# A recurrence and two MLPs on one core: the weight conversion as six lagged stages, the second MLP's weights kept in SBUF, and a mask product taken by VectorE from PSUM

## Chip, core and metric

The kernel runs on one core of a Trainium2 chip. The metric is the device time of one execution in microseconds (us). The core's engines are TensorE (PE, its weight loads PEld), VectorE (DVE), ScalarE (ACT), GpSimd (POOL) and SyncE (SP, which here only issues DMAs). Each engine works through its own queue in program order; they meet at semaphores.

## The reference

Three steps follow each other. A recurrence over 768 time steps for 4 batches of 8 heads with 40 channels, then two MLPs over its 3072 rows of 320 columns:

```python
for t in range(S):
    y[:, :, t] = einsum('bhd,bhde->bhe', rt, state)
    Sa = einsum('bhde,bhe->bhd', state, at)
    state = state * wt[:, :, None, :] - einsum('bhd,bhe->bhde', Sa, bt) + einsum('bhd,bhe->bhde', vt, kt)
...
h = x @ moe_w_in;  x = (maximum(h, 0) ** 2) @ moe_w_out            # 320 -> 2048 -> 320
h = x @ moe2_w_in; out = (h * clip(h + 3, 0, 6) / 6) @ moe2_w_out
```

The weights come as 64-bit floats. The kernel gets them as pairs of 32-bit words (low word, high word) and has to turn each pair into a 32-bit float itself.

## The kernel before

**The recurrence** is cut into 12 chunks of 64 steps with 4 batches each: 48 units, `i` = 0 to 47. In the main loop one iteration treats one unit; its words come from `ORDER` (`ORDER0` until the first MLP has input). Products of decayed rows for unit `i + 8` are made in `f1` (L581, eight matmuls): `f1a` copies one half to `TB`, which goes to DRAM (`DT`) and feeds a triangular inverse; `f1b` treats the other half: ScalarE copies 64x256 out of the bank to `RK` (L595), GpSimd multiplies it there by a mask (L596). It is done 96 times, twice for each unit; the first eight units go through it ahead of the loop. A chunk's inverse (`inv_gen`, L627 and L630, 62 small steps in a row on VectorE) is spread over the loop by `tick()`; only that of chunk 1 runs on GpSimd. `ys` (L710, L713 on PE, then L717, L719, L722 on VectorE) gives the rows of a unit.

**The MLPs** run in *pieces*. Their tokens are six groups of 512, the 2048 hidden columns 16 blocks of 128: 96 blocks for each MLP. An "in" piece multiplies one block into the hidden layer (L221 to L225), applies the function (first MLP L235 to L239, second L230 to L239); an "out" piece multiplies it with the second weight and adds it up (first L248 to L252, second L260 to L262). Operands are taken in a high and a low part, so that each product is three. The word `M` of the order calls `fill`, which issues one piece (or `keep_warm`, matmuls that nobody reads, where there is none), then up to five ticks, and two steps of the conversion. The first MLP begins in iteration 9; four `M` in an iteration make two blocks. After the loop pieces follow each other without recurrence; the first MLP's last group and all of the second MLP run there.

**The conversion** (`convert`, a generator) turns 32 items (16 blocks of both weights, 128x384 or 128x320) of one MLP. An item goes through VectorE (L127, L135), ScalarE (L130, and |high word| in L126 or L138), GpSimd (L139, integer add), VectorE (L146), then `split`: ScalarE rounds to the high part (L70, L74), GpSimd or VectorE subtracts (L156), and the low part is stored to DRAM (`LI`, `LO`). The high parts stay in SBUF (`wi_hi`, `wo_hi`); low parts are loaded back for every group, two blocks in a tile `wl` (L169, issued from ScalarE's queue). Of the first MLP's items 16 are converted in iterations 0 to 7. The other 16 put their low parts directly into the tiles from which the first group reads them (`wd`), so each waits until the first group is two blocks away ("held"). All 32 of the second MLP are such: they are held until the first MLP is at its last blocks. `need` runs the generator on where a block asks for an item that isn't there.

Of the kernel before, what the change touches and what calls it, by code (L numbers as in the profile page):

```python
# [33 lines left out]
class Moe:  # L34


    def __init__(self, tc, ctx, pctx, consts):
# [7 lines left out]
        self.pso4, self.gpool, self.depth = None, self.rot, 2  # L45
# [3 lines left out]
        self.pairs = {}  # L49
# [4 lines left out]
    def weights(self, pool, dram, second, rot):  # L54


        w = {"second": second, "rot": rot, "in": pool.tile([128, NF, 3, 128], F32R, name="wi_hi"),
             "out": pool.tile([128, NF, DM if second else 256], F32R, name="wo_hi")}
        w["li"], w["lo"] = ([dram.tile([128, 2, 384], FP32, name=f"{n}{second}_{k}") for k in range(NF // 2)]
                            for n in ("LI", "LO"))  # L60
        return w

    def split(self, w, part, f, raw, t):

        nc = self.nc
        n = 384
        if part == 0 or w["second"]:
            n = DM if part else 384
            hi = w["out"][:, f] if part else w["in"][:, f].rearrange("p k c -> p (k c)")
            nc.scalar.copy(out=hi, in_=raw)  # L70
            self.low(t[:, 0:n], raw, hi, nc.vector if part else nc.gpsimd)
        else:
            hi = w["out"][:, f]
            nc.scalar.copy(out=hi, in_=raw[:, 0:256])  # L74
            nc.scalar.copy(out=t[:, 0:64], in_=raw[:, 256:320])
            self.low(t[:, 128:384], raw[:, 0:256], hi, nc.vector)
            self.low(t[:, 64:128], raw[:, 256:320], t[:, 0:64], nc.vector)
        (nc.sync if part else nc.gpsimd).dma_start(out=w["lo" if part else "li"][f // 2][:, f % 2, 0:n], in_=t.bitcast(FP32)[:, 0:n])

    def convert(self, w, w_in, w_out, scratch, first, direct):  # L80

# [6 lines left out]
        todo = deque()  # L88
        order = [(f, part) for q in range(0, NF, 2) for part in range(2) for f in (q, q + 1)]

        def load(k):
            f, part = order[k]
            bits = scratch(k, 0)[:, 0:640 if part else 768]
            nc.sync.dma_start(out=bits, in_=(w_out if part else w_in)[f])
            return bits.rearrange("p (c w) -> p c w", w=2)

        count = [0, 0]

        def fill():

            while count[0] < len(order) and count[0] - count[1] < scratch(count[0], 2):
                todo.append(load(count[0]))
                count[0] += 1

        fill()
        yield
        late = []
        for k, (f, part) in enumerate(order):
            n = DM if part else 384
            if f >= direct and f % 2 == 0:  # L110

                while (self.n_out if part else self.n_in) < first + f - 2:
                    if late:
                        late.pop()()
                    yield "held"
                self.pairs[w["second"], part, f] = w["rot"].tile([128, 2, 384], F32R, tag=("wi", "wo")[part], name="wd")
            own = scratch(k, 3)
            fill()
            bits = todo.popleft()
            low, high = bits[:, :, 0], bits[:, :, 1]  # L120
            t = scratch(k, 1)[:, 0:n]

            q, m = (x[:, 0:n] for x in own) if own else (low, high)
            q, m = q.bitcast(I32), m.bitcast(FP32)
            if own:
                nc.scalar.activation(out=m, in_=high.bitcast(FP32), func=ACTF.Abs)  # L126
# [326 lines left out]
def rwkv_moe_moe2_kernel(ctx, tc, pre_in, vr_in, v_in, nat, ident_d, mask_d, cst_d, w1_in, w1_out, w2_in, w2_out, out,  # L453
# [384 lines left out]
    with tc.manual_schedule():  # L838
# [146 lines left out]
        def scratch2(k, what):  # L985
            if what == 2:
                return 4
# [92 lines left out]
```

## Time and profile before

| what | value |
|---|---|
| median of three runs | 1441.65 us (1439.43 to 1443.51) |
| the profiled execution | 1440.75 us, of which 1439.0 us lie between its first and last instruction (the span) |
| mean granted TensorE clock | 0.895 of full speed |
| PE busy | 1186.5 us (82%) |
| VectorE busy | 792.5 us (55%) |
| ScalarE busy | 610.6 us (42%) |
| GpSimd busy | 409.4 us (28%) |
| moved by DMA | 178.43 MB |

Busy times of PE are modelled: its matmuls overlap, so that a busy PE isn't yet PE at its peak. A share over the whole span mixes stages that are bounded by different things. The profile's wait lists name an instruction that began late, what its engine waited for, and how long in total, how often, and the longest.

### The profile page before, as it was taken

The page shows a single profiled execution, that of the slowest core. Times are in us where ns is not written, and L with a number is a line of the kernel's source. Part 1 is how long each engine was busy: PE and PEld are TensorE (multiplying, and loading weights), DVE is VectorE, ACT ScalarE, POOL GpSimd, SP SyncE. Part 2 cuts the span into 40 slices and gives each one's busy share as a digit, 9 for nine tenths or more (in the row PEclk, how much of TensorE's full clock was granted, in tenths as well). Part 3 has the DMA queues.
Part 4 walks back from the last instruction along what each step waited for, and adds up shares of the span by engine and source line. Part 5 has one row for each costly group of instructions (what it writes and reads, how often), then busy time and mean ns, then how long its engine had stood idle before and what let it go on. Part 6 is the DMA issues. An engine that isn't in the chain of part 4 may idle for free.

```text
span 1439.0 us, 25925 instructions
## 1 busy us (share of the span) xinstructions
PE 1186.5 (82%) x9682; PEld 1003.3 (70%) x9682; DVE 792.5 (55%) x1841; ACT 610.6 (42%) x1456; POOL 409.4 (28%) x612
## 2 busy tenths in 40 slices
PE   3177787976679899999999899797666899999994
PEld 3166776855568677777778778585544798888984
DVE  7823667586575949575765733345554444344432
ACT  4144443535445445445444433344444433344331
POOL 5685454344534333333332000003333000000000
PEclk9668689987689999999999999898778999999997
DMA  5534556636537475665655442634333443434331
GB/s 127 135 79 132 124 123 141 145 94 145 131 95 164 104 143 150 138 122 137 140 133 107 128 111 76 213 110 149 121 112 99 135 130 118 138 104 136 102 118 50
DMA packets 270150, 178.43 MB, mean 124 GB/s; under 512 B 202944, under 2 KB 228160, under 8 KB 270016
## 3 DMA queue, kind: packets, MB, share of 16 engines
q1 hardware_dynamic: 238656, 106.95, 32.5%
q10 hardware_dynamic: 29312, 63.45, 14.7%
q0 software_dynamic: 2048, 6.29, 1.1%
q8 instruction: 79, 1.29, 0.4%
q14 instruction: 55, 0.45, 0.1%
HBM read 140.99 MB, written 35.65 MB: 123 GB/s over the span
## 4 chain that ended last, share of the span: by engine, by line
PE 36%; DVE 13%; DMA 11%; ACT 4%; POOL 3%; issue 3%; SPq 1%; ACTq 0%; DVEq 0%; POOLq 0%
PE h L221 7%; PE h L223 3%; PE o L261 3%; DMA DT<-TB 3%; DMA wl<-LO 3%; PE o L262 3%; DMA wl<-LI 3%; PE o L260 2%; DVE TMP L627 2%; DVE INV L630 2%; PE o L248 2%; POOL cv L139 2%; PE h L225 2%; PE h L224 2%; PE o L250 2%
## 5 line engine op out<-in xcount | busy, mean ns | idle before, releaser
L221 PE MATMUL h<-xm,wi_hi 128*128 128x512 f32 x384 | 165.9, 432 | 38.5 <-ACT wi_hi L70 38.5
L239 DVE TENSOR_TENSOR gs<-g,gs 128x512 fp32r<-128x512 f32 x192 | 143.8, 749 | 80.7 <-ACT gs L233 68.8
L221 PE MATMUL h<-xm,wl 128*128 128x512 f32 x336 | 134.5, 400 | 22.5 <-DMA wl<-LI 22.5
L627 DVE TENSOR_TENSOR TMP<-ML,INV 128x126 f32<-128x126 f32 (+22 forms) x341 | 109.7, 322 | 70.1 <-DMA ML<-DT 50.9
L596 POOL TENSOR_TENSOR RK<-RK,mask 64x256 f32<-64x256 f32 x96 | 74.0, 771 | 255.6 <-ACT RK L595 244.4
L231 DVE SCALAR_TENSOR_TENSOR g<-r,h 128x512 f32<-128x512 f32 x96 | 65.9, 686 | 124.5 <-ACT r L230 124.4
L236 DVE TENSOR_TENSOR g<-r 128x512 f32<-128x512 f32 x96 | 66.6, 694 | 112.1 <-ACT r L235 112.1
L260 PE MATMUL o<-wo_hi,gs 128*128 128x320 f32 x384 | 123.0, 320 | 4.8 <-ACT os L822 3.0
L262 PE MATMUL o<-wo_hi,gs 128*128 128x320 f32 x384 | 122.6, 319 | 1.9 <-DVE gs L239 1.9
L223 PE MATMUL h<-xr,wi_hi 128*128 128x512 f32 x384 | 123.2, 403 | 0.0
L230 ACT ACTIVATE r<-h,cst 128x512 f32<-128x512 f32 x96 | 66.0, 687 | 122.2 <-PE h L225 117.8
L139 POOL TENSOR_TENSOR cv<-bits,cv 128x384 int32<-128x384 int32 (+1 forms) x48 | 44.7, 931 | 254.2 <-DVE bits L127 183.4
L221 PEld LDWEIGHTS h<-xm,wi_hi 128*128 128x128 f32 x384 | 76.9, 200 | 49.9 <-ACT wi_hi L70 40.5
L630 DVE TENSOR_TENSOR INV<-INV,TMP 128x126 f32<-128x126 f32 (+22 forms) x341 | 106.7, 313 | 7.9
L235 ACT ACTIVATE r<-h 128x512 f32<-128x512 f32 x96 | 57.2, 596 | 104.7 <-PE h L225 95.1
L261 PE MATMUL o<-wl,gs 128*128 128x320 f32 x320 | 99.9, 312 | 0.4
L233 ACT CAST gs<-g 128x512 fp32r<-128x512 f32 x96 | 59.5, 620 | 71.7 <-DVE g L231 71.7
L221 PEld LDWEIGHTS h<-xm,wl 128*128 128x128 f32 x336 | 64.1, 191 | 34.9 <-DMA wl<-LI 26.6
L223 PEld LDWEIGHTS h<-xr,wi_hi 128*128 128x128 f32 x384 | 75.1, 196 | 17.6
L248 PE MATMUL o<-gs,wo_hi 128*128 128x512 f32 x192 | 86.9, 452 | 0.0
L557 POOL TENSOR_TENSOR RK<-IN,EE 40x256 f32<-40x256 f32 x82 | 69.8, 852 | 57.6 <-DVE EE L545 54.3
L260 PEld LDWEIGHTS o<-wo_hi,gs 128*128 128x128 f32 x384 | 74.9, 195 | 14.1 <-ACT gs L233 6.6
(174 smaller groups left out, 2763.8 us busy)
## 6 DMA issues: line engine op xcount, KB each, us to landing
wl<-LI ACTq DMA_DIRECT2D x84, 384.0 KB
IN<-in_pre_dram SPq DMA_DIRECT2D x44, 418.0 KB
wl<-LO ACTq DMA_DIRECT2D x44, 384.0 KB
wl<-LO ACTq DMA_DIRECT2D x40, 320.0 KB
bits<-in_moe_w_in_dram SPq DMA_DIRECT2D x32, 384.0 KB
bits<-in_moe_w_out_dram SPq DMA_DIRECT2D x32, 320.0 KB
VR<-in_vr_dram SPq DMA_DIRECT2D x96, 80.0 KB
DT<-TB SPq DMA_DIRECT2D x24, 256.0 KB
```

Of the source, the lines that this page charges most:

```text
L139: nc.gpsimd.tensor_tensor(out=q, in0=t.bitcast(I32), in1=q, op=ALU.add)
L221: nc.tensor.matmul(h, w[p][:, k], xm[:, k], start=(k + p == 0), stop=False)
L223: nc.tensor.matmul(h, hi[:, k], lo[:, k], start=False, stop=False)
L239: nc.vector.tensor_tensor(out=gs[:, 1], in0=g, in1=gs[:, 0].bitcast(FP32), op=ALU.subtract)
L248: nc.tensor.matmul(acc[d], hi, gs[:, 0], start=a, stop=False)
L260: nc.tensor.matmul(acc[q], gs[:, 0, s], hi, start=a, stop=False)
L261: nc.tensor.matmul(acc[q], gs[:, 0, s], lo[:, 0:DM], start=False, stop=False)
L262: nc.tensor.matmul(acc[q], gs[:, 1, s], hi, start=False, stop=z)
L557: e.tensor_tensor(out=rk[P, :, 64 * h:64 * h + 64], in0=a[P], in1=E[P, :, 0:64], op=ALU.mult)
L596: nc.gpsimd.tensor_tensor(out=o, in0=o, in1=mask[P].unsqueeze(1).to_broadcast([64, NP, 64]), op=ALU.mult)
L627: eng.tensor_tensor(out=tmp, in0=ml[:, s, s + 1:32].unsqueeze(2).to_broadcast([128, n, w]), in1=inv[:, s, 0:w].unsqueeze(1).to_broadcast([ ...
L630: eng.tensor_tensor(out=inv[:, s + 1:32, 0:w], in0=inv[:, s + 1:32, 0:w], in1=tmp, op=ALU.subtract)
```

## The change

The conversion becomes a pipeline in six stages. A step of the generator loads item r + 1 and runs stage 1 of item r, stage 2 of item r - 1, and so on to stage 6 of item r - 5; 32 items take 38 steps. The first MLP's 32 items are all converted ahead of its first group, one step in each `M` in place of two; their low parts all go to DRAM, and VectorE makes all of them. The second MLP's low parts stay in SBUF beside the high ones (`resident`), so nothing of it is loaded for a group; its conversion starts as the loop ends, with one step for each piece, while the first MLP's last group runs. Its converted floats are also stored to DRAM in full, for `general_path` alone, which these inputs don't enter. `f1b` becomes one VectorE product from the bank for each half. Three buffers for the function's results come from two pools, the input tiles of the second MLP from those of the first, and outputs have three buffers in place of four.

```diff
@@ class Moe
-    def split(self, w, part, f, raw, t):
...
+    def resident(self, w, pool):
+        for n in ("in", "lin"):
+            w[n] = pool.tile([128, NF, 3, 128], F32R, name=f"w2_{n}")
+        for n in ("out", "lout"):
+            w[n] = pool.tile([128, NF, DM], F32R, name=f"w2_{n}")
-    def convert(self, w, w_in, w_out, scratch, first, direct):
+    def convert(self, w, w_in, w_out, scratch):
...
+        def load(k):
+            f, part = order[k]
+            bits[k] = scratch("bits", k)[:, 0:2 * n_of[part]]
+            nc.sync.dma_start(out=bits[k], in_=(w_out if part else w_in)[f])
...
+        def first(k):
+            low, high = views(k)
+            t = res[k] = scratch("res", k)[:, 0:n_of[order[k][1]]]
+            nc.scalar.mul(out=low.bitcast(I32), in_=low, mul=2.0 ** -29)
             nc.vector.tensor_scalar(out=t, in0=high, scalar1=0x07FFFFFF, scalar2=3, op0=ALU.bitwise_and,
                                     op1=ALU.logical_shift_left)
             nc.vector.scalar_tensor_tensor(out=t, in0=high, scalar=0xC0000000, in1=t, op0=ALU.bitwise_and,
                                            op1=ALU.bitwise_or)
+        def second(k):
+            low, high = views(k)
+            nc.scalar.activation(out=high.bitcast(FP32), in_=high.bitcast(FP32), func=ACTF.Abs)
+            nc.gpsimd.tensor_tensor(out=low.bitcast(I32), in0=res[k].bitcast(I32), in1=low.bitcast(I32), op=ALU.add)
+        def third(k):
+            low, high = (x.bitcast(FP32) for x in views(k))
+            nc.vector.scalar_tensor_tensor(out=res[k].bitcast(FP32), in0=high, scalar=TINY, in1=low, op0=ALU.is_ge,
+                                           op1=ALU.mult)
+            del bits[k]
+        def fourth(k):
+            f, part = order[k]
+            v, hi = res[k].bitcast(FP32), high_of(k)
+            if w["second"]:
+                nc.sync.dma_start(out=w["full"][f][:, 384 * part:384 * part + n_of[part]], in_=v)
+            else:
+                rest[k] = scratch("rest", k).bitcast(F32R)
+                if part:
+                    nc.scalar.copy(out=rest[k][:, 0:64], in_=v[:, 256:320])
+            nc.scalar.copy(out=hi, in_=v if w["second"] or part == 0 else v[:, 0:256])
+        def fifth(k):
+            f, part = order[k]
+            v, hi = res.pop(k).bitcast(FP32), high_of(k)
+            if w["second"]:
+                self.low(w["lout"][:, f] if part else w["lin"][:, f].rearrange("p k c -> p (k c)"), v, hi,
+                         nc.vector if part else nc.gpsimd)
+            elif part == 0:
+                self.low(rest[k], v, hi, nc.vector)
+            else:
+                self.low(rest[k][:, 128:384], v[:, 0:256], hi, nc.vector)
+                self.low(rest[k][:, 64:128], v[:, 256:320], rest[k][:, 0:64], nc.vector)
+        def sixth(k):
+            f, part = order[k]
+            if not w["second"]:
+                nc.sync.dma_start(out=w["lo" if part else "li"][f // 2][:, f % 2], in_=rest.pop(k).bitcast(FP32))
+            self.converted = k + 1
+        n = len(order)
+        load(0)
+        yield
+        for r in range(n + 5):
+            if r + 1 < n:
+                load(r + 1)
+            for lag, stage in ((5, sixth), (4, fifth), (3, fourth), (2, third), (1, second), (0, first)):
+                if 0 <= r - lag < n:
+                    stage(r - lag)
             yield
...
     def block_in(self, w, f):
+        if w["second"]:
+            self.need(w, 2 * (f - f % 2) + 4)
+            return w["in"][:, f], w["lin"][:, f]
...
     def prep(self):
+        if self.raw is self.plan[0][1]:
+            for _ in self.aside:
+                pass
@@ f1b
-            nc.scalar.copy(out=o, in_=ps[P, :, 64 * h:64 * h + 64])
-            nc.gpsimd.tensor_tensor(out=o, in0=o, in1=mask[P].unsqueeze(1).to_broadcast([64, NP, 64]), op=ALU.mult)
+            s = slice(64 * h, 64 * h + 64)
+            nc.vector.tensor_tensor(out=rk[P, :, s], in0=ps[P, :, s],
+                                    in1=mask[P].unsqueeze(1).to_broadcast([64, NP, 64]), op=ALU.mult)
@@ main loop and what follows it
                     for k in range(5):
                         tick()
-                        if k < 2:
-                            cstep(1)
+                    cstep(1)
...
-            if i == 2 * NB - 1:
-                moe.need(raw1, n_early)
...
-        moe.aside, moe.steps = moe.convert(raw2, w2_in.bitcast(U32), w2_out.bitcast(U32), scratch2, NG * NF, 0), 2
-        cstep(9)
+        moe.aside = moe.convert(raw2, w2_in.bitcast(U32), w2_out.bitcast(U32),
+                                lambda what, k: cv2.tile([128, 768 if what == "bits" else 384], U32, tag=what, name=what))
+        moe.steps = 1
+        cstep(2)
```

The conversion's scratch has four buffers for the words (`bits`) and four for the results (`res`) in both MLPs.

## Rows read from the trace of the kernel before

**Rows 1.** Stretches: us, then each engine's busy us (instructions), clock, DMA share, GB/s.

```profile
core 0: us, PE busy (x) PEld busy (x) DVE busy (x) ACT busy (x) POOL busy (x), PEclk, DMA share, GB/s
72.00:247.00 175.00, 137.59 (x1491) 123.99 (x1491) 90.55 (x249) 75.36 (x224) 98.29 (x153) 0.77 0.51 118
144.00:252.00 108.00, 86.09 (x934) 77.38 (x935) 73.51 (x207) 46.35 (x139) 52.59 (x76) 0.80 0.57 130
299.00:430.00 131.00, 90.42 (x803) 74.98 (x803) 91.15 (x227) 63.50 (x166) 59.94 (x77) 0.77 0.49 118
430.00:758.00 328.00, 302.62 (x3138) 250.05 (x3137) 224.80 (x586) 160.49 (x435) 121.80 (x185) 0.96 0.61 136
468.00:504.00 36.00, 30.73 (x319) 25.16 (x316) 33.02 (x97) 15.41 (x43) 12.29 (x18) 0.95 0.41 104
900.00:920.00 20.00, 9.82 (x39) 7.73 (x38) 6.01 (x9) 5.24 (x9) 0.00 (x0) 0.77 0.85 242
920.00:978.00 58.00, 58.00 (x255) 47.98 (x254) 25.81 (x41) 23.63 (x41) 3.62 (x4) 0.99 0.38 132
978.00:1112.00 134.00, 86.01 (x311) 65.50 (x311) 69.68 (x139) 61.83 (x126) 49.89 (x59) 0.75 0.37 121
1194.00:1254.00 60.00, 58.22 (x321) 51.95 (x321) 25.27 (x38) 23.18 (x37) 0.00 (x0) 1.00 0.43 126
```

**Rows 2.** PE in order of time: first instruction of iterations 13, 18 and 38 (start, duration).

```profile
299.55 0.67 PE L670 MATMUL a<-VS,RK 128*64 128x40 f32 x16
...
429.83 0.67 PE L670 MATMUL a<-VS,RK 128*64 128x40 f32 x16
...
757.04 0.67 PE L670 MATMUL a<-VS,RK 128*64 128x40 f32 x16
```

**Rows 3.** Waits in 299 to 430 us: total us, times, longest.

```profile
PE a L680 <- ACT RHS L672: 28.0, 5, 6.1
ACT bits L138 <- DVE cv_t L135: 25.6, 12, 6.4
```

**Rows 4.** PE in order of time: resuming after the loop, and the last matmul of the MLPs.

```profile
917.72 0.80 PE L221 MATMUL h<-xm,wl 128*128 128x512 f32 x1 [10.18 <-DMA wl<-LI]
...
1420.38 0.31 PE L262 MATMUL o<-wo_hi,gs 128*128 128x320 f32 x1
```

**Rows 5.** The chain that ended last: the same place of two second-MLP blocks, eleven blocks apart.

```profile
1204.63 0.93 PE h L221 x4
...
1244.16 0.93 PE h L221 x4
```

**Rows 6.** Waits in 978 to 1112 us.

```profile
DVE cv L146 <- POOL cv L139: 38.9, 28, 3.1
PE h L221 <- ACT wi_hi L70: 38.5, 7, 8.6
```

**Rows 7.** Waits in 72 to 247 us.

```profile
DVE bits L156 <- DMA LO<-bits: 13.2, 2, 7.0
...
PE a L710 <- ACT cv L130: 10.9, 2, 7.6
```

**Rows 8.** Groups by line and shape: count, busy us, mean ns, then idle before.

```profile
L596 POOL TENSOR_TENSOR RK<-RK,mask 64x256 f32<-64x256 f32 x96 | 74.0, 771 | 255.6 <-ACT RK L595 244.4 <-issue 7.3
...
L719 DVE TENSOR_TENSOR XT<-a,EE 104x256 f32<-104x256 f32 x48 | 19.9, 415 | 8.3 <-PE a L713 8.3
```

**Rows 9.** VectorE in order of time, inverse of chunk 0.

```profile
37.99 0.19 DVE L627 TENSOR_TENSOR TMP<-ML,INV 128x31 f32<-128x31 f32 x1 [1.47 <-DMA ML<-DT]
...
41.25 0.76 DVE L630 TENSOR_TENSOR INV<-INV,TMP 128x78 f32<-128x78 f32 x1
...
57.30 0.24 DVE L630 TENSOR_TENSOR INV<-INV,TMP 128x78 f32<-128x78 f32 x1
```

**Rows 10.** PE in order of time: end of `ys` and `f1` of iteration 18.

```profile
433.33 0.64 PE L713 MATMUL a<-VR,SB 40*40 40x64 f32 x16
...
434.35 1.16 PE L581 MATMUL a<-RK,KBt 104*128 104x128 f32 x8
```

## What I expected of the change

> **What bounds the kernel now.** I first read the busy times by stretch [rows 1]. From 430 to 758 us, recurrence and first MLP together, PE is busy 302.6 of 328 us at clock 0.96; from 920 to 978 us all the time; from 1194 to 1254 us 58.2 of 60. Those stretches are bounded by PE. Three are not: 72 to 247 us (PE 137.6 of 175, clock 0.77), 299 to 430 us (90.4 of 131, clock 0.77) and 978 to 1112 us (86.0 of 134, clock 0.75). In none is another engine full, so they are bounded by waits, and in each the old conversion runs. In the last two PE waits for a weight's high part (38.5 us, 7 times), and VectorE for GpSimd's add of the same item (38.9 us) [rows 6]; and, between 299 and 430 us, PE waits for `RHS`, a copy that stands behind conversion in ScalarE's queue, which itself waits there for VectorE (28.0 and 25.6 us) [rows 3]. One item's chain crosses three engines, and each of them waits in order with the MLP's or the recurrence's work queued behind it. I then read how long each stretch would take without that.
>
> **Second MLP's conversion.** From 917.72 to 1420.7 us [rows 4] PE has 112 blocks left, 16 of the first and 96 of the second MLP. A block of the second takes (1244.16 - 1204.63) / 11 = 3.594 us [rows 5], one of the first 58.0 / 16 = 3.63 [rows 1], together 58.1 + 345.0 = 403.1 us. The stretch takes 503.0: 99.9 us are idle or at half clock. Most are in 978 to 1112, 134 us for 16 blocks that need 57.5; the rest are waits for `wl` between groups (60 us in place of 57.5 for a group [rows 1]) and those just after the conversion.
>
> The change puts the conversion beside the first MLP's last group. Its 38 steps meet 2 in `cstep` and some 34 pieces until the second MLP's first block, which needs 4 items: `need` has nothing to run. What must fit there:
> - VectorE: 69.7 us for 16 blocks and the conversion without its first items [rows 1]. Those I take as 3 us, near the 3.6 that GpSimd has of them before 978 us. Two blocks more until the last step, at 25.27 / 16 = 1.6 each: 69.7 + 3 + 3.2 = 76 us (an estimate from these rows).
> - ScalarE: 61.8 [rows 1] and the same additions, 67 us. GpSimd 49.9 and 3.6: 54.
> - DMA: the words, 16 x (384 + 320) KB = 11.5 MB; the full floats, half of that; `wl` of a first-MLP group, 16 x 384 KB = 6.3 MB; some 1.5 MB of inputs and outputs: 25.1 MB. At the rate of 978 to 1112 us scaled to a full share, 121 / 0.37 = 327 GB/s, 77 us; at the 242 GB/s reached from 900 to 920 us [rows 1], 104.
> - PE: 18 blocks, 65 us.
>
> Four users within 65 to 77 us, all with in-order queues, don't overlap perfectly. I take 90 us, halfway from 77 to 104: 25 of the 99.9 us stay, and 1 us for the third output buffer (the fourth copy of a group waits for a store). Gain 74 us; bounds: 3 us stay (all hidden), 97; 45 stay, 55. The group edges are in this sum: nothing is loaded there any more. What is late next is VectorE, or a load of words that has two steps' time to land.
>
> **First MLP's late half.** Iterations 13 to 17 take 429.83 - 299.55 = 130.3 us; the next 20 take (757.04 - 429.83) / 20 = 16.36 each [rows 2], and five of those are 81.8. The change has no conversion there, so the stretch falls to what follows it: gain 48.5 us. The added loads of low parts for that group (8 tiles) are those that every later group already has beside the same work.
>
> **First MLP's early half.** Here 32 items are converted in the place of 16, four in an iteration. The steps are as many as there are `M` until the first group is prepared, so the program's order of the first block doesn't move. VectorE: the second MLP's rows give (69.7 - 25.8 + 3) / 32 = 1.5 us an item; the low parts that GpSimd made before add, scaled by columns from 0.415 us for 256 [rows 8], 0.62 for half of the items: 1.8. So 4 x 1.8 = 7.2 in place of 2 x 1.5 = 3.0, and 0.83 for two products of `f1b` at 0.415 each: 5.0 us more in each iteration. From 144 to 252 us are six iterations: 73.5 + 30 = 104 of 108 us [rows 1]. VectorE is nearly full there. On the other side go the waits of the old items: VectorE for a store of `LO` 13.2 us, PE's `ys` behind a conversion's ScalarE work 10.9 [rows 7]; in the new order a store has two steps until its buffer is written again. I take +3 us, between -20 (these waits, with some clock) and +25 (VectorE 90% efficient at best, and its waits for PE). SP gets more loads in an iteration, but its queue holds no more than a step's.
>
> **The product from the bank.** It takes 96 GpSimd products (771 ns) and 96 ScalarE copies away and gives VectorE 96 products, priced by the nearest row, a VectorE product of 256 columns from a bank, 0.415 us [rows 8]: 0.83 an iteration. In VectorE's queue it stands behind `ys`'s three operations, and behind it stand the scans and the mask of `GV`, for which `ys` of the next iteration waits; the bank stays taken until VectorE comes to it. Ahead of the loop 16 products are 6.6 us on VectorE before the first inverse, which had 1.47 us to wait anyway [rows 9]. Against that, an inverse step of 78 columns took 0.76 us while GpSimd's masks ran and 0.24 without [rows 9]: eight masks of units 4 to 7, 6.2 us, are some 8 slowed steps, 4.2 us back. VectorE must now wait there for PE's `f1`, up to 1.16 us at full clock [rows 10], for four units; I take 2 us in all: 6.6 - 1.5 - 4.2 + 2 = +3 us (-3 to +8). In the loop VectorE is busy 69% from 430 to 758 us, but 33.0 of 36 from 468 to 504 [rows 1], where an inverse runs. I take half of the iterations for such; there 0.83 is added, and some 0.5 comes back as masks no longer slow the inverse: +0.3 for 20 iterations, +6 us (-10 to +33, the last if nothing comes back and all 40 iterations pay 0.83).
>
> Here a page speaks against this edit. The Trainium skill, Perfetto Trace Analysis, section Optimizing Scalar/DVE Operations, advises moving work off VectorE where it is saturated; it adds that GpSimd may not help, as the two share a read port. By its first half the edit costs 33 us instead of 6; the slowed step in rows 9 bears out the second half.
>
> **Sum** for the profiled execution, 1440.75 us (0.9 below the median): -74 - 48.5 + 3 + 3 + 6 = -110.5, so 1330 us.
>
> **Rivals.**
> - The second conversion hides fully, 3 us left: 1306. For it: no single engine needs over 77 us. Against: four nearly equal users.
> - Transfers pace it, 104 us: 1344. For it: share 0.85 gave only 242 GB/s. Against: that stretch had many small rows of the inputs.
> - VectorE saturates in iterations 0 to 9: +25, 1352 with +3 replaced. For it: 104 of 108 us. Against: the whole of 72 to 247 us holds 90.55, so its first half is far emptier.
> - VectorE's product unhidden in every iteration, +33: 1357. The page above would have it so.
> - Slower than before: VectorE's queue stalls at the product until PE has done `f1`, in all 48 units, with everything behind it late. From the end of `ys` to that of `f1` PE needs 1.54 us [rows 10], with the product 2.4; at half clock 3.9. With half clock in one of three iterations 2.9 us, 139 in all in place of my 9: 1460. It decides from 119.5 / 48 = 2.5 us a unit. Against: `ys`'s own operations, and ticks of the inverse between them, fill most of that time.
> - The change doesn't do what it says: the second conversion starts so late (memory the loop leaves, buffers) that `need` still runs it before each block: the 74 us don't come, 1404.
>
> **Chances.** Forecast 60% (1312 to 1348), hidden 12%, transfers 5%, early saturation 12%, unhidden product 6%, slower 3%, not as said 2%. The range 1300 to 1364 holds all but the last two and the ends of the others. A measurement of this kernel can tell some 0.3%, 4 us, from no change: faster by more 0.96, within 0.01, slower 0.03.
>
> **What would show it.** Right: no PE wait for a high part at the second MLP's start, GpSimd busy before 960 us in the first MLP's last group, groups of the second MLP at 57.5 us, iterations 13 to 17 at some 16 us each. Wrong: a stretch around the last first-MLP group far over 90 us, with waits on VectorE or on `bits` loads; the stretch that is 72 to 247 us now longer than 175 us; `st` or `ys` waiting for VectorE in every iteration; PE's clock at half in the new conversion stretch.

## The result, and where the time went

The changed kernel takes 1399.44 us (median of four runs, 1394.85 to 1400.25) where the kernel before takes 1442.58: ratio 0.9696, 95% interval 0.9667 to 0.9725. It is faster, by 43 us instead of the 110 forecast, and lies 35 us above the upper end of the range. The profiled execution is the one of 1394.85 us, with a span of 1393.1.

Marks in the two traces say where. They are the first instruction of an iteration (PE's `rhs`, L670 before, L675 after) and the last "in" matmul of an MLP block (L225 before, L226 after; blocks count from 0, 96 and up are the second MLP's; a group is 16 blocks):

| stretch | before, us | after, us | change | forecast |
|---|---|---|---|---|
| start to iteration 0 | 71.9 | 78.3 | +6.4 | +3 |
| iterations 0 to 9 | 175.4 | 193.6 | +18.2 | +3 |
| iterations 10 to 12 | 52.2 | 56.1 | +3.9 | in the +6 for the loop |
| iterations 13 to 17 | 130.3 | 79.8 | -50.5 | -48.5 |
| iterations 18 to 47 | 453.3 | 455.3 | +2.0 | in the +6 |
| iteration 47 to block 80 | 37.3 | 31.7 | -5.6 | none |
| blocks 80 to 112 | 192.7 | 159.1 | -33.6 | -53 |
| blocks 112 to 176, four groups | 245.4 | 256.6 | +11.2 | -15 |
| block 176 to the end | 80.5 | 82.7 | +2.2 | -3 |

The forecasts of the last three are worked out from its terms: two groups at 57.5 us and 25 that stay, then groups at 57.5. They come to 71 of the 74 us forecast for the second conversion.

The rows of three of these starts, beside [rows 2]; PE in order of time, start and duration:

```profile
271.86 0.67 PE L675 MATMUL a<-VS,RK 128*64 128x40 f32 x16
...
327.91 0.49 PE L675 MATMUL a<-VS,RK 128*64 128x40 f32 x10
...
407.66 0.55 PE L675 MATMUL a<-VS,RK 128*64 128x40 f32 x12
```

The stretches of the changed kernel that answer to [rows 1] (us, busy us and instructions of each engine, clock, DMA share, GB/s):

```profile
78.00:272.00 194.00, 145.83 (x1505) 130.98 (x1502) 146.15 (x351) 92.85 (x262) 81.33 (x126) 0.70 0.61 152
328.00:408.00 80.00, 75.35 (x792) 62.50 (x792) 60.12 (x165) 37.89 (x100) 20.61 (x32) 0.96 0.57 132
408.00:736.00 328.00, 300.54 (x3114) 248.15 (x3110) 233.15 (x625) 150.31 (x392) 90.35 (x146) 0.95 0.60 136
894.60:992.00 97.40, 74.40 (x258) 57.87 (x257) 90.22 (x137) 60.61 (x124) 53.13 (x45) 0.82 0.76 236
1066.00:1126.00 60.00, 59.19 (x320) 53.39 (x320) 25.28 (x38) 23.18 (x37) 0.00 (x0) 0.97 0.08 27
```

The second and third row are what the forecast said: PE full, clock 0.96. The fourth is the new conversion stretch, where VectorE, the third figure, is busy 90.2 of 97.4 us; the first is the early part, at clock 0.70 in place of 0.77, VectorE busy 146 us in place of 90.6. In the last row DMA is nearly idle, and a group still takes 64 us. The loss is at its edge, where one group's sums are copied out and stored and the next group begins. Waits from 1055 to 1135 us (two edges), and PE in order of time:

```profile
DVE os L837 <- DMA out_dram<-os: 10.5, 2, 5.3
...
PE o L261 <- DVE os L837: 8.3, 2, 4.2
```

```profile
1062.31 0.31 PE L263 MATMUL o<-w_out,gs 128*128 128x320 f32 x1
1066.81 0.63 PE L261 MATMUL o<-w_out,gs 128*128 128x320 f32 x1 [4.20 <-DVE os L837]
```

The fourth copy of a group waits 5.3 us until the first copy's store has landed and its buffer is free; PE's next group needs the bank that this copy reads, and waits 4.2. Behind the gap PE runs at the lower of its two clocks for a while (0.63 us for a matmul that took 0.31); stretches before and behind it:

```profile
1050.00:1062.00 12.00, 12.00 (x69) 10.91 (x68) 4.54 (x7) 5.19 (x9) 0.00 (x0) 1.00 0.34 88
1066.80:1072.00 5.20, 5.19 (x20) 4.57 (x21) 1.52 (x3) 1.31 (x2) 0.00 (x0) 0.68 0.15 52
```

So an edge costs the wait and some 2 us more (6.6 us, as the fourth buffer below shows). The chain that ended last crosses each edge by that store:

```profile
1060.22 5.93 DMA out_dram<-os
...
1123.72 5.86 DMA out_dram<-os
```

### The profile page after: what moved, and what is told of

The parts are those of the page before. It is cut to its first block, busy times and chain, and to the rows that moved or that the text cites. A ratio compares the mean times of both kernels' runs of the same rounds, so it can differ in the third digit from the quotient of the medians.

```text
span 1393.1 us, 25861 instructions
## 1 busy us (share of the span) xinstructions
PE 1177.7 (85%) x9682; PEld 1004.1 (72%) x9682; DVE 857.2 (62%) x1953; ACT 587.0 (42%) x1360; POOL 307.7 (22%) x468
## 4 chain that ended last, share of the span: by engine, by line
PE 48%; DMA 19%; DVE 18%; SPq 4%; issue 4%; POOL 3%; ACT 2%; DVEq 0%; ACTq 0%; POOLq 0%
PE h L222 9%; DMA DT<-TB 6%; PE h L224 4%; PE o L261 4%; PE o L262 4%; PE o L263 4%; DVE TMP L632 3%; DVE INV L635 3%; DMA out_dram<-os 3%; PE h L225 2%; PE h L226 2%; PE o L249 2%; SPq L622 2%; DMA W<-res 2%; PE a L586 2%
## 5 line engine op out<-in xcount | busy, mean ns | idle before, releaser
L240 DVE TENSOR_TENSOR gs<-g,gs 128x512 fp32r<-128x512 f32 x192 | 150.4, 783 | 77.5 <-ACT gs L234 65.9
L261 PE MATMUL o<-w_out,gs 128*128 128x320 f32 x384 | 120.9, 315 | 22.8 <-DVE os L837 20.6
L562 POOL TENSOR_TENSOR RK<-IN,EE 40x256 f32<-40x256 f32 x82 | 58.3, 711 | 355.3 <-DVE EE L550 323.9
L105 POOL TENSOR_TENSOR bits<-res,bits 128x384 int32<-128x384 int32 (+1 forms) x64 | 70.0, 1095 | 233.3 <-DMA wl<-LI 123.4
L263 PE MATMUL o<-w_out,gs 128*128 128x320 f32 x384 | 119.9, 312 | 0.0
L262 PE MATMUL o<-w_lout,gs 128*128 128x320 f32 x384 | 119.9, 312 | 0.0
L222 PE MATMUL h<-xm,wl 128*128 128x512 f32 x192 | 80.6, 420 | 26.4 <-DMA wl<-LI 26.4
L234 ACT CAST gs<-g 128x512 fp32r<-128x512 f32 x96 | 59.5, 620 | 97.4 <-DVE g L232 97.4
L261 PEld LDWEIGHTS o<-w_out,gs 128*128 128x128 f32 x384 | 73.5, 191 | 28.6 <-DVE os L837 21.9
L249 PE MATMUL o<-gs,wo_hi 128*128 128x512 f32 x192 | 89.4, 465 | 3.5 <-ACT os L827 2.1
L222 PE MATMUL h<-xm,wi_hi 128*128 128x512 f32 x192 | 86.0, 448 | 0.6 <-ACT xm L208 0.6
L577 POOL TENSOR_TENSOR KBt<-IN,RV 104x256 f32<-104x256 f32 x78 | 77.5, 1012 | 36.6 <-DVE TMP L632 12.6
L250 PE MATMUL o<-gs,wo_hi 128*128 128x512 f32 x192 | 81.6, 425 | 0.7 <-DVE gs L240 0.7
L251 PE MATMUL o<-gs,wl 128*128 128x512 f32 x192 | 81.2, 423 | 0.2 <-DMA wl<-LO 0.2
L715 PE MATMUL a<-GV,KT 128*64 128x104 f32 (+1 forms) x768 | 49.5, 276 | 34.7 <-DVE GV L696 34.7
```

Source lines behind the costliest of these rows:

```text
L105: nc.gpsimd.tensor_tensor(out=low.bitcast(I32), in0=res[k].bitcast(I32), in1=low.bitcast(I32), op=ALU.add)
L222: nc.tensor.matmul(h, w[p][:, k], xm[:, k], start=(k + p == 0), stop=False)
L240: nc.vector.tensor_tensor(out=gs[:, 1], in0=g, in1=gs[:, 0].bitcast(FP32), op=ALU.subtract)
L249: nc.tensor.matmul(acc[d], hi, gs[:, 0], start=a, stop=False)
L250: nc.tensor.matmul(acc[d], hi, gs[:, 1], start=False, stop=False)
L251: nc.tensor.matmul(acc[d], lo, gs[:, 0], start=False, stop=z)
```

## Experiments

Times are medians of four runs (of two where said), ratios are against the kernel before on the same chip, with their 95% interval. The kernel before took 1435.5 to 1442.6 us (medians) in the five batches of runs, so a difference of a few us between two batches is read from the ratios or from marks within the traces. Three questions: the edges, the conversion stretch, the early part.

**A fourth output buffer.**

```diff
-                o = opool.tile([128, DM], FP32, name="os")
+                o = (opool.tile([128, DM], FP32, name="os") if q < 3
+                     else moe.rot.tile([128, DM], FP32, tag="wi", name="os"))
```

> The changed kernel with a fourth output buffer for the second MLP (the fourth copy of a group goes to a buffer of the first MLP's weights, idle by then). Theory, the third buffer holds the group edges: the fourth copy no longer waits for a store (31.5 us in all), each of the five edges falls from 64 us a group to some 60, as before the change, and the time from 1399 to about 1375 to 1380. Rival, the edge is set by the next group's inputs or by the order of the four copies: groups stay at 64 us and the time within 4 us of 1399.

1362.76 us, ratio 0.9494 (0.9445 to 0.9543). Blocks 112 to 176 take four times 57.5 us in place of 256.6 in all, block 176 to the end 77.1 in place of 82.7: 32.2 us in these marks. From 1060 to 1290 us PE is busy without a gap:

```profile
1060.00:1290.00 230.00, 230.00 (x1282) 208.51 (x1281) 101.11 (x153) 92.63 (x149) 0.00 (x0) 1.00 0.08 26
```

The theory holds and was too small: the groups don't go back to the 60 us of before but to 57.5, what their blocks alone take. The diffs below leave this edit out where a run has it besides.

**The stores of the full floats after the conversion.**

```diff
-            if w["second"]:
-                nc.sync.dma_start(out=w["full"][f][...], in_=v)
...
+        for f in range(NF if w["second"] else 0):
+            for part, names in enumerate((("in", "lin"), ("out", "lout"))):
+                for j, name in enumerate(names):
...
+                    nc.sync.dma_start(out=w["full"][f][...], in_=x.bitcast(FP32))
+                yield
```

> The changed kernel with the second MLP's full floats not stored item by item during the conversion; their two parts are stored from SBUF after it, one a step, while the second MLP computes (the general path adds them). Theory, these stores pace the conversion (VectorE's first operation of an item waits until the store of the item four before has landed, and the loads of the first MLP's low parts share the transfers): the 116 us from the 80th to the 97th MLP block fall to about 95, the time to about 1380. Rival, VectorE and the in-order queues pace it: the stretch stays within 5 us and the time too. A second rival: the later stores lengthen the edges of the second MLP, which takes back what is gained.

1398.61 us, 0.9731 (0.9684 to 0.9779): no change. Blocks 80 to 96 took 94.2 in place of 97.3 us, the next group 66.8 in place of 61.8. From 896 to 992 us VectorE was busy 91.6 of 96 us. What PE itself waits for in the stretch is a DMA, though: the first MLP's low parts (waits from 890 to 1005 us, of the changed kernel, then of this run):

```profile
PE h L222 <- DMA wl<-LI: 23.5, 6, 5.5
```

```profile
PE h L226 <- DMA wl<-LI: 21.9, 6, 4.5
```

In the changed kernel PE goes on 4.7 to 6.4 us after such a load is issued (five of the six waits), in this run 2.8 to 3.4. So without the stores the loads are faster, and PE's wait stays: the load is issued late, from ScalarE's queue, where ScalarE waits 35 us for VectorE's results in the same window. The amount of transfers did not set the pace.

**GpSimd's subtractions to VectorE.** What VectorE does there was the next question. Groups by line and shape, 894.6 to 992 us of the changed kernel (count, busy us, mean ns), then GpSimd's:

```profile
L240 DVE TENSOR_TENSOR gs<-g,gs 128x512 fp32r<-128x512 f32 x15 | 17.9, 1194 | 2.0
L109 DVE SCALAR_TENSOR_TENSOR res<-bits 128x384 f32<-128x384 f32 x15 | 14.1, 939 | 0.0
L154 DVE TENSOR_TENSOR w_lout<-res,w_out 128x320 fp32r<-128x320 f32 x14 | 12.9, 920 | 0.0
L99 DVE SCALAR_TENSOR_TENSOR res<-bits,res 128x384 uint32<-128x384 uint32 x15 | 11.9, 791 | 0.5
...
L97 DVE TENSOR_SCALAR res<-bits 128x384 uint32<-128x384 uint32 x14 | 8.2, 584 | 3.2 <-DMA W<-res 3.1
```

```profile
L154 POOL TENSOR_TENSOR w_lin<-res,w_in 128x384 fp32r<-128x384 f32 x15 | 19.2, 1278 | 1.1 <-ACT w_in L122 1.1
L105 POOL TENSOR_TENSOR bits<-res,bits 128x384 int32<-128x384 int32 x15 | 18.7, 1244 | 22.3 <-DVE res L99 18.2 <-ACT w_out L122 2.6 <-ACT gs L238 0.9
```

The same operations in the old conversion stretch of the kernel before, 978 to 1112 us, where VectorE and GpSimd took turns, and L240 of the changed kernel in the second MLP, 1200 to 1260 us, where GpSimd does nothing:

```profile
L146 DVE SCALAR_TENSOR_TENSOR cv<-cv 128x384 f32<-128x384 f32 x14 | 7.8, 558 | 27.8 <-POOL cv L139 27.8
L135 DVE SCALAR_TENSOR_TENSOR bits<-bits 128x384 uint32<-128x384 uint32 x14 | 7.7, 551 | 0.0
...
L156 DVE TENSOR_TENSOR wd<-cv,wo_hi 128x320 fp32r<-128x320 f32 x14 | 6.9, 493 | 7.3 <-ACT wo_hi L70 7.3
...
L127 DVE TENSOR_SCALAR bits<-bits 128x384 uint32<-128x384 uint32 x14 | 4.9, 353 | 0.0
```

```profile
L240 DVE TENSOR_TENSOR gs<-g,gs 128x512 fp32r<-128x512 f32 x16 | 11.1, 693 | 11.0 <-ACT gs L234 11.0
```

The five grew by 0.50, 0.38, 0.43, 0.24 and 0.23 us each, together 26 us (15 x 0.50 + 15 x 0.38 + 14 x 0.43 + 15 x 0.24 + 14 x 0.23), while GpSimd had 45 operations: 0.58 us of VectorE for each. One such meeting, GpSimd and VectorE in order of time:

```profile
892.17 1.27 POOL L105 TENSOR_TENSOR bits<-res,bits 128x384 int32<-128x384 int32 x1 [123.43 <-DMA wl<-LI]
```

```profile
892.65 1.33 DVE L240 TENSOR_TENSOR gs<-g,gs 128x512 fp32r<-128x512 f32 x1
```

GpSimd's ends at 893.44, VectorE's 0.54 us behind it at 893.98, though it began 0.79 us before that end and takes 0.69 alone. This agrees with the Trainium skill, SBUF — State Buffer, section "SBUF: two separate sides", by which a GpSimd operation and a VectorE operation with two inputs in SBUF exclude each other for a whole instruction. The run moves GpSimd's subtractions to VectorE:

```diff
                 self.low(w["lout"][:, f] if part else w["lin"][...], v, hi,
-                         nc.vector if part else nc.gpsimd)
+                         nc.vector)
```

> The changed kernel with the fourth output buffer, and with the low parts of the second MLP's input weights (16 subtractions of 384 columns) made by VectorE in the place of GpSimd. In the 97.3 us from the 80th to the 96th block VectorE is busy 93%, and its operations are longer than elsewhere (0.94 us in place of 0.56 for 384 columns, 1.19 in place of 0.69 for 512). Theory, a GpSimd operation stretches the VectorE operations beside it by about as much as VectorE would need for the work itself: VectorE has 16 operations more, the others get shorter, and the stretch stays at 97 us or falls to 91; time 1356 to 1363. Rival, VectorE's own number of operations decides and the longer ones are of another cause: 16 x 0.55 us more, stretch at 105 to 111, time about 1372.

1363.48 us, 0.9465 (0.9425 to 0.9506). Blocks 80 to 96 took 93.7 us in place of 97.3, with 16 VectorE operations more; the group after took 1.8 more, and the time stayed within the interval. L154 for 320 columns is back at 0.52 us:

```profile
L154 DVE TENSOR_TENSOR w_lin<-res,w_in 128x384 fp32r<-128x384 f32 x14 | 7.7, 548 | 0.0
L154 DVE TENSOR_TENSOR w_lout<-res,w_out 128x320 fp32r<-128x320 f32 x13 | 6.8, 521 | 0.0
```

The rival, that VectorE's own number of operations decides, asked for 105 us or more and is out. With the 30 GpSimd operations that are left VectorE's grew by 17.5 us in all, 0.58 us for each again; and as the transfers ran at 242 GB/s, against 236, they did not stretch them. A subtraction of 384 columns costs VectorE 0.55 us if it does it, and some 0.58 if GpSimd does.

**The second conversion over more blocks.**

```diff
-        for _ in range(self.steps):
+        self.beat += self.steps
+        while self.beat >= 3:
+            self.beat -= 3
             next(self.aside, None)
```

> The changed kernel with the fourth output buffer, and with two steps of the second conversion for three pieces of MLP work in place of three: the conversion runs on into the second MLP, over some 26 blocks instead of 18. Theory, VectorE's work for the stretch is too much for the 16 blocks (5.6 us a block with two items, PE needs 3.6), and it is the same work that would fit beside more blocks: about 4.2 us of VectorE a block, the stretch from the 80th to the 112th block falls from 160 us to about 138, time 1335 to 1345. Rival, the loss comes from each item's chain over three engines (a fixed loss an item, wherever it is): the same 45 us are lost over more blocks, the two groups stay at 155 to 162 us, time within 5 us of 1363.

With `moe.steps` at 2. 1348.53 us, 0.9365 (0.9327 to 0.9402). Blocks 80 to 96 take 73.6 us, 96 to 112 70.6: 144.1 in place of 160.0. The loss is no fixed price of an item; it is VectorE's work in too few blocks, which reaches PE through ScalarE's late loads. Less was won than expected (138): PE still waits 9.8 us there for `wl` of the first MLP.

**The early part: loads, masks, GpSimd.** Waits of the changed kernel from 78 to 272 us, and the longest pieces of the chain from 76 to 135 us that aren't the inverse:

```profile
ACT bits L96 <- DMA bits<-in_moe_w_out_dram: 56.2, 14, 8.5
...
DVE res L97 <- DMA bits<-in_moe_w_out_dram: 32.6, 9, 6.8
PE a L715 <- DVE GV L696: 31.8, 8, 6.3
```

```profile
94.08 4.72 DMA bits<-in_moe_w_out_dram
...
107.12 2.26 SPq L645
...
112.95 3.71 DMA bits<-in_moe_w_out_dram
...
132.19 4.65 DMA bits<-in_moe_w_out_dram
```

A load is issued one step before its use, behind whatever SP's queue holds (here the inverse's tiles, L645), and ScalarE and VectorE stand at the head of their queues until it lands. PE feels it in `ys` (L715), where it waits 31.8 us in ten iterations until VectorE has come to the mask of `GV`. The run loads three items ahead, in six places (a place is a buffer for one item):

```diff
-            if r + 1 < n:
-                load(r + 1)
+            if r + 3 < n:
+                load(r + 3)
```

> The changed kernel with the words of the first MLP's conversion loaded three items ahead instead of one, in six places instead of four. Theory, late loads: ScalarE stands 56 us in iterations 0 to 9 at the head of its queue until words have landed, the recurrence's copies behind it; this goes, iterations 0 to 9 fall from 193.6 us to about 178 and the time to about 1384. Rival, VectorE's added work (146 of 194 us busy): the wait moves to VectorE, iterations 0 to 9 stay above 189 and the time within 4 us of 1399.

1392.64 us, 0.9692 (0.9643 to 0.9742): the ratio is that of the changed kernel (0.9696), and iterations 0 to 9 took 191.3 us, 2.3 less. In the main the rival holds. ScalarE's wait for words was gone, and the next transfer of the same item took its place, low parts whose places are written again one step after their store is issued (waits, 78 to 270 us of this run):

```profile
DVE rest L156 <- DMA LI<-rest: 29.2, 5, 7.8
...
ACT rest L121 <- DMA LO<-rest: 20.5, 3, 7.9
```

The old product everywhere (ScalarE copies, GpSimd masks):

> The changed kernel with the old product of decayed rows: ScalarE copies it from the bank and GpSimd masks it. By the prediction's terms the new form costs 3 us ahead of the loop and 6 in it: 1390, of which 3 ahead of the first iteration. Rival one, the new form is most of what the early stage lost: first iteration at 73 instead of 78 us and iterations 0 to 9 some 10 us shorter, 1380. Rival two, the new form gains in the loop, as ScalarE and GpSimd are freed: iterations 18 to 37 longer than 328.5 us, the time 1400 to 1415.

1397.63 us, 0.9734 (0.9686 to 0.9781): none of the three. Iteration 0 began at 71.7 in place of 78.3 us, and iterations 0 to 9 took 200.2 in place of 193.6. In iterations 18 to 37 the new product costs 4.6 us (328.5 against 323.9), in 38 to 47 it gains 5.0 (126.8 against 131.8). The other kernels with the new product lie at 328.1 to 331.0 and 125.9 to 129.5, the kernel before, with the old one, at 327.2 and 126.1, so the second difference isn't the product's alone. The ratios (0.9734 against 0.9696 with the new product) have overlapping intervals: the whole edit can't be told from nothing. PE's wait for `GV` in iterations 0 to 9 is there with the old product too (36.9 us), so it isn't the new product that brings it.

All low parts of the first MLP on GpSimd:

> The changed kernel with the fourth output buffer, and with the low parts of the first MLP's weights (48 subtractions, 25.4 us of VectorE in iterations 0 to 9) made by GpSimd. Theory, VectorE's number of operations sets the early iterations: 193.7 us for iterations 0 to 9 fall to about 175. Rival, the operations moved to GpSimd stretch VectorE's others by as much: 188 to 198 us, time 1357 to 1368.

1367.45 us, 0.9488 (0.9452 to 0.9525), iterations 0 to 9 at 199.1 us: 48 operations fewer on VectorE and 5.4 us longer than with the fourth buffer alone. VectorE's busy time fell by 5.2 us (144.4 to 139.2) and not by the 24.2 of these operations, so each of the 48 cost it some 0.40 us on GpSimd; besides, it now waited 16.0 us until GpSimd had read a buffer.

The old product for the eight units ahead of the loop alone:

```diff
+            if i < lag:
+                nc.scalar.copy(out=rk[P, :, s], in_=ps[P, :, s])
+                nc.gpsimd.tensor_tensor(out=rk[P, :, s], in0=rk[P, :, s], in1=mask..., op=ALU.mult)
+                continue
```

> The changed kernel with the fourth output buffer, and with the old product (ScalarE's copy, GpSimd's mask) for units 0 to 7 alone, ahead of the loop; all later units keep VectorE's product. Theory, VectorE stands 7.8 us ahead of the loop at these products until PE has done a unit's matmuls at half clock, and the first inverse starts at 47.2 in place of 38.0 us: the first iteration starts at 72 instead of 78.5 us and all else moves with it, time about 1356. Rival, iterations 0 to 9 take the 6.5 us back, as they did when all products had the old form (200.2 in place of 193.6 us): time within 2 us of 1363.

1362.48 us, 0.9452 (0.9415 to 0.9489). Iteration 0 began at 72.0, and iterations 0 to 9 took 200.9: iteration 10 began at 272.8, as with VectorE's product (272.2). What was ready earlier ahead of the loop waited in it; which wait took the 6.5 us back isn't shown.

**Is it the transfers or the arithmetic?** On the kernel with the fourth buffer and the spread conversion, whose iterations 0 to 9 take 193.2 us: words two items ahead and three pairs of places for low parts; the first conversion's arithmetic left out; its loads left out.

```diff
-            if r + 1 < n:
-                load(r + 1)
+            if r + 2 < n:
+                load(r + 2)
...
+                places[0] = (moe.rot.tile([128, 2, 384], U32, tag="wo", name="rest") if k // 2 % 3 < 2
+                             else extra()[:, 768:].rearrange("p (a b) -> p a b", a=2))
```

> The changed kernel with the fourth output buffer and the second conversion at two steps for three pieces; besides, in the first MLP's conversion words are loaded two items ahead (five places) and the low parts wait for their stores in three pairs of places instead of two. Theory, the transfers' delays pace the early iterations: with loads three ahead alone ScalarE's 56 us of waits for words were gone, but VectorE and ScalarE then waited 29 and 21 us until low parts had been stored; with both out of the way iterations 0 to 9 fall from 193 us to 180 or less, time 1336 or less. Rival, the engines' work itself (VectorE with GpSimd beside it) sets them: 189 to 194 us, time 1345 to 1349.

> The changed kernel with the fourth output buffer and the second conversion at two steps for three pieces; of the first MLP's conversion the arithmetic is left out (an item has one copy on VectorE in place of three operations, none of ScalarE's first two, no GpSimd add); its loads, its high and low parts and its stores stay. Theory, engine work sets the early iterations: without some 40 us of VectorE and 33 of GpSimd, iterations 0 to 9 fall from 193 us to 165 to 175, as before the change or less. Rival, the transfers and the queue that issues them set them: 186 to 193 us.

> The changed kernel with the fourth output buffer and the second conversion at two steps for three pieces; of the first MLP's words only those of four items are loaded (28 loads are left out, their items use the words of the first four); all arithmetic and all stores stay. Theory, engine work: iterations 0 to 9 stay at 188 to 194 us. Rival, loads that take time and places in the queue that issues them: 180 us or less.

Deeper places: 1337.80 us, 0.9310 (0.9276 to 0.9344), iterations 0 to 9 at 182.8. Arithmetic left out (two runs): 1332.11 us, iterations 0 to 9 at 173.3. Loads left out (two runs): 1335.03 us, 181.2. The stretch with deeper places, then without arithmetic:

```profile
78.00:261.00 183.00, 144.76 (x1503) 130.12 (x1501) 150.29 (x353) 93.21 (x260) 83.30 (x126) 0.73 0.62 160
```

```profile
78.00:251.00 173.00, 139.24 (x1492) 125.94 (x1491) 95.50 (x285) 63.72 (x196) 45.04 (x92) 0.76 0.67 170
```

Neither theory alone: the transfers' delay is worth 10.4 us, with no byte less moved, and the arithmetic 19.9. Leaving out 28 of the 32 loads wins little more (12.0) than deeper places do. One trace stands behind each of these; kernels with the same early part differ by up to 3 us (182.8, 184.4 and 181.2 us with deeper places). With both (the joined kernel below, arithmetic left out, two runs, 1317.94 us):

> The joined kernel with the arithmetic of the first MLP's conversion left out (one copy on VectorE an item; loads, parts and stores stay). If transfers and arithmetic are two causes that add, iterations 0 to 9 fall from the 182.8 us with deeper buffers to about 163 (193 less 10 less 20). If they are one cause (an item's chain, of which each is a part), they stay at 170 to 175.

Iterations 0 to 9 at 166.7 us, against 184.4 with the arithmetic: between two causes that add in full (163) and one (170 to 175). Together they took 26.5 us off the 193.2, of 30.3 if they added, so they are two causes that overlap in small part.

**Together.** The first join had the loads three ahead without the third pair of places; the second has both, and the last also the late stores of the full floats:

> The changed kernel with the fourth output buffer, the second conversion at two steps for three pieces, the low parts of the second MLP's input weights made by VectorE, and the first MLP's words loaded three items ahead. From the single runs: 1348.5, some 3 us less from GpSimd's subtractions (the stretch from the 80th to the 96th block was 93.7 in place of 97.3 us), some 4 to 6 less from the earlier loads: 1339 to 1343. Rival: the gains of the first group come back in the next, as they did with the subtractions alone, and the early loads only move a wait: 1346 to 1349.

> The edits that helped, together: the changed kernel with the fourth output buffer, the second conversion at two steps for three pieces, the low parts of the second MLP's input weights on VectorE, and the first conversion with words two items ahead and three pairs of places for low parts. From the single runs, 1337.8 and some 3 us less in the first two groups around the second conversion (141.2 in place of 144.6 us): 1333 to 1336. Rival: the subtractions cost VectorE what they save, 1337 to 1339.

> The joined kernel with the full floats of the second MLP stored in two parts from SBUF after the conversion. With VectorE's load spread, the first MLP's low parts still come late in that stretch (PE waits 10 us for them). If the stores share the transfers with them: the two groups from the 80th block fall by 5 to 8 us. If VectorE still sets the pace: within 2 us. The later stores come beside the second MLP, whose edges have four buffers now and should stay at 57.5 us a group.

1341.09 us, 0.9323 (0.9294 to 0.9352); 1332.65, 0.9274 (0.9234 to 0.9315); 1328.67, 0.9260 (0.9217 to 0.9303). The first two came out within half a microsecond of their forecasts. The late stores, worth nothing while VectorE set the pace, took 3.8 us off blocks 80 to 96 (69.8 us) once it didn't, between the two forecasts; PE's waits for `wl<-LI` fell from 14.0 to 7.5 us. The two ratios overlap, so the whole time doesn't show this gain beyond doubt. This version beats both kernels. And the mask ahead of the loop once more, on the second join:

> The joined kernel with the old product for units 0 to 7 alone, ahead of the loop. If the 6.5 us gained there were lost again because iterations 1 to 9 waited for the conversion's transfers, they stay now, at least in part: first iteration at 72, iterations 0 to 9 at 182 to 185, time some 5 us below the joined kernel's. If what ends the early part is the sum of the engines' work until the first weights are ready, they are lost again: iterations 0 to 9 at 188 to 190, time within 2 us.

1332.36 us, 0.9280 (0.9240 to 0.9321). In its trace iteration 10 begins at 256.2 us, against 259.5 to 263.0 in the three traces with deeper places and VectorE's product, so at least part of the gain stayed there; but the median (1332.65 without this edit) doesn't show it. What the product ahead of the loop is worth in the end stays open.

## Why the forecast was right in part

The profiled execution came 65 us above the forecast (1394.85 against 1330). Three terms of its sum failed, and they make up that difference: the third output buffer (1 us, measured 32), the second conversion (25 us to stay, measured 45) and the early half (+3 us, measured +18.2). The rest nearly cancels. Two readings of the forecast are wrong without changing a term: [rows 6] are of 978 to 1112 us alone, and from 299 to 430 us PE's list has no wait for a high part; and the first rival adds up to 1307, not 1306. Point by point:

- **Iterations 13 to 17**, -48.5 forecast, -50.5 measured. Right, and for the reason given: the stretch fell to the rate of the iterations behind it, 16.0 us each.
- **The third output buffer** was the largest error: a term of 1 us that measured 32. The prediction names the mechanism (the fourth copy waits for a store) and gives it no row. The store takes 5.9 us to land, the other copies cover little of that, and PE pays some 4.2 us of idle time and some 2 at the lower clock at each of five edges; the sixth such wait delays the last copy of the kernel. I forecast groups at 57.5 us; they were 64, and 57.5 with the fourth buffer.
- **The second conversion**, 25 us to stay of its 99.9, of which some 45 stayed (blocks 80 to 112 with four buffers: 160.0 us, two groups at 57.5 are 115). The wrong term is VectorE's 76 us. Its durations came from a stretch in which VectorE and GpSimd waited for each other in turn [rows 6], so that the conversion's operations hardly met; side by side each GpSimd operation costs VectorE 0.58 us. For the 16 blocks of that stretch, 64 us of work became 90. The effect itself stood in my own rows: an inverse step at 0.76 us beside GpSimd's masks and 0.24 without [rows 9]. I used it for the masks and not for the conversion. The rival "transfers pace it" had the better time for the stretch (104 us, where the 65 of PE's work and the 45 that stay make 110) for the wrong reason: with the stores out of the stretch it kept its length.
- **The early half**, +3 forecast, +18.2 measured, inside the bounds of -20 to +25 but far from the value taken. I gave it VectorE's work (5.0 us more in an iteration; its busy time grew by 5.6) and set against nearly all of it the waits that would go. The new order had waits of its own instead, loads one step ahead and low-part places written again one step behind their stores, where I had counted two; they are worth 10.4 us. PE's `ys` waits for VectorE's `GV` 8 times in the ten iterations, which was one of my signs of being wrong. "Its queue holds no more than a step's" was the wrong test: a load is late not because SP holds more of them but because it is issued a step before use, behind the inverse's tiles.
- **The product ahead of the loop**, +3 forecast, +6.4 measured. The 2 us for VectorE's waits were too few. VectorE in order of time:

```profile
32.35 0.86 DVE L600 TENSOR_TENSOR RK<-a,mask 64x256 f32<-64x256 f32 x2 [2.33 <-ACT TB L589]
34.79 0.86 DVE L600 TENSOR_TENSOR RK<-a,mask 64x256 f32<-64x256 f32 x2 [1.58 <-ACT TB L589]
...
44.02 0.86 DVE L600 TENSOR_TENSOR RK<-a,mask 64x256 f32<-64x256 f32 x2 [2.34 <-ACT TB L589]
46.46 0.86 DVE L600 TENSOR_TENSOR RK<-a,mask 64x256 f32<-64x256 f32 x2 [1.58 <-ACT TB L589]
47.24 0.17 DVE L632 TENSOR_TENSOR TMP<-ML,INV 128x31 f32<-128x31 f32 x1
```

  Four waits, 7.8 us, and the first inverse starts at 47.24 in place of 37.99 us [rows 9]. PE's `f1` of a unit takes 1.95 to 2.05 us here, not the 1.16 of [rows 10]: the clock from 22 to 45 us is 0.50. Each wait ends with ScalarE's two copies of the same bank to `TB` (L589, 0.74 us), which begin as PE ends; the forecast had only PE's part. This is the mechanism of the "slower" rival, but it stayed small: in the whole trace these products wait 27.6 us, 13 times, of which 16.0 in the five waits up to 82 us.
- **The product in the loop**, +6 forecast for its iterations. Iterations 18 to 47 show +2.0 against before; against the old product in the changed kernel 18 to 37 show +4.6 and 38 to 47 -5.0. The +6 is neither borne out nor ruled out. The whole edit, +9 by my terms, is 1.8 us by the medians (1399.44 against 1397.63) and the other way by the ratios (0.9696 against 0.9734): not told from nothing. It isn't the 33 us of the rival.

## To carry to other kernels

Price a buffer that is taken away by the landing time of the store that frees it, less the work that covers it, and multiply by how often it comes round. Take an engine's durations from a stretch in which its neighbour worked as it will after the change; durations from two engines that took turns are too short for the two side by side. In a pipeline of lagged stages look at the first and the last stage: a load or a store that has one step until its buffer is needed makes every in-order queue behind it wait.

## What the hardware showed that I had not expected

- GpSimd's help was free in neither conversion: in the second a GpSimd operation of 1.1 to 1.3 us cost VectorE 0.58 us, as much as the same subtraction on VectorE (0.55); in the first, some 0.40.
- A 160 KB store took 5.8 to 5.9 us to land, with two more issued behind it, in a stretch where the DMA engines were 8% busy (27 GB/s).
- A gap of 4.2 us cost PE 6.6 us a group (64.2 against 57.5): matmuls behind it took 0.63 in place of 0.31 us.
- An earlier start of the loop by 6.5 us did not bring iteration 10 forward (272.8 against 272.2 us).
